# First three projection chains interleaved over K, memory products on three PSUM banks, the second remainder tile loaded in stage one

## The chip, the cores and the metric

The kernel runs on one NeuronCore of a Trainium2 chip. Its metric is the device time of that core in microseconds (us). A core has a matrix engine (TensorE, in the profile PE, with its weight loads as PEld), a vector engine (VectorE, DVE), an activation engine (ScalarE, ACT), a general engine (GpSimd, POOL), and a queue from which this kernel issues all its transfers (SyncE, SP). SBUF is the working memory. PSUM holds the matrix results: eight banks, each of 128 partitions by 512 float32 numbers.

## The reference, cut to what matters

The input `x` has 2048 rows and 576 columns. Two results are made from it and mixed row by row with `g = sigmoid(x . gate_w)`:

```
q, k, v = x @ wq, x @ wk, x @ wv            # 32 heads of 18, four segments of 512 rows
for each segment s:
    a_dot = softmax(q k^T * scale + causal mask) v      # inside the segment
    a_mem = (phi(q) M) / (phi(q) z + 1e-6)              # memory of the segments before
    M, z += phi(k)^T v, sum phi(k)
    o = sigmoid(beta) * a_mem + (1 - sigmoid(beta)) * a_dot
a = o @ wo
b = (silu(x @ w_gate) * (x @ w_up)) @ w_down            # 4608 hidden units
out = g * a + (1 - g) * b
```

The kernel computes float32 products from pairs: a number is split into a high part (a copy on ACT in a rounded type) and a low part (the difference, on DVE), and a product is high*high + high*low + low*high.

## The kernel before, in words

Every engine runs its instructions in the order in which the program lists them; the order of the work is written out by hand. A tile has a name, and each name has a fixed place (or a few, used in turn). A new tile under a name waits until the last reader of the tile that lay there is done. PSUM is used under eight names, `bank0` to `bank7`, and helpers such as `chain_tile = banks(0, 1, 2)` hand them out in turn.

Stage one goes through the four segments (`for s in range(NSEG)`, L562). A segment consists of two phases.

- **Nine chains** (L565, `qk`, L315). A chain makes 128 columns of q or k for the 512 rows of the segment. The 576 input columns are five K blocks (`NT = 5`; the last block is a half one that holds high and low part together). A chain is 14 matmuls of 512 columns into one bank (`products`, L134): three for each of four blocks, two for the last. Chain 0 to 4 are the (m, 0), chain 5 to 8 the (m, 1). When a chain is done it is evacuated: ACT copies it to 16 bits (L320), for some chains ACT makes `phi` from it (L325, L326), DVE takes the rest (L327), `mid` work follows, ACT copies the rest (L330), POOL takes what then is left (L331), and for the `phi` chains DVE reads the bank once more (L333). That last read frees the bank. The result is stored to DRAM two chains later (`flush`, L312).
- **Eight V steps** (L623, `v_step`), each of 14 matmuls of 288 or 290 columns, on banks 5, 6 and 7. From the second segment on a **memory step** (`mem_step`, L410) follows each V step: six short matmuls into one bank taken from `pair_tile = banks(3, 4)`, and four DVE instructions (L424 to L428) that read it. Between the chains of these segments `upd_gen` (L367) updates the memory M, with its sums in the same two banks.

At the very start the weights of chain 0 (all five blocks, 320 KB) are loaded, then x block by block (five transfers of 256 KB), then the weights of chain 1, 2, 3 and so on. ACT and DVE split weights and x in that order; the weights of chain n + 3 are split inside the evacuation of chain n. While the first data is on its way, nine matmuls on zeros run on PE (L437).

Stage two (from L659) is the feed-forward part in two halves of 36 steps f, with the attention heads worked in between. Its step makes seven products (`seven`) on `a_tile` (bank 0), `x_tile` (bank 1) and `y_tile` (bank 2); the first is on bank 0, the second on bank 2. Each product ends with one matmul (L1014) on a remainder tile `rh` that `r_fetch(f)` (L234) loads from DRAM; there are two such tiles. `r_fetch(0)` is issued in the last segment of stage one, the others inside stage two, one step ahead, from a list that is worked off beat by beat.

Few lines say how the memory step takes its bank:

```
            t = pair_tile([P, 16, E])                       # L417, mem_step
            acc = [pair_tile([P, 3, MW]), pair_tile([P, 2, MW])]   # L368, upd_gen
    y_tile = banks(2)                                       # L109
```

## Time and profile before

| what | value |
|---|---|
| median of three runs | 1793.36 us (1793.08 to 1793.77) |
| the profiled execution's own time | 1792.96 us |
| its span, first to last instruction | 1791.2 us |
| PE busy | 1775.8 us (99%) |
| DVE, ACT, POOL busy | 1268.9, 959.3, 830.9 us |
| stage one | about 0 to 222 us |
| granted TensorE clock | 1.00 |

All times inside the profile count from the first instruction of the span. A row of the timeline gives start, duration, engine, line of the kernel, operation, output and inputs, and in brackets how long the engine sat idle before it and what released it. `xcount` tells how many instructions were merged into the row. Matmuls overlap: one of 512 columns has a duration of 0.39 us, while a new one starts each 0.23 us. So a stall of PE is read from the starts of rows rather than from the busy share.

### The profile page before, as it was taken

The page shows a single profiled execution, that of the slowest core. Times are in us where ns is not written, and L with a number is a line of the kernel's source. Part 1 is how long each engine was busy: PE and PEld are TensorE (multiplying, and loading weights), DVE is VectorE, ACT ScalarE, POOL GpSimd, SP SyncE. Part 2 cuts the span into 40 slices and gives each one's busy share as a digit, 9 for nine tenths or more (in the row PEclk, how much of TensorE's full clock was granted, in tenths as well). Part 3 has the DMA queues.
Part 4 walks back from the last instruction along what each step waited for, and adds up shares of the span by engine and source line. Part 5 has one row for each costly group of instructions (what it writes and reads, how often), then busy time and mean ns, then how long its engine had stood idle before and what let it go on. Part 6 is the DMA issues. An engine that isn't in the chain of part 4 may idle for free.

```text
span 1791.2 us, 36353 instructions
## 1 busy us (share of the span) xinstructions
PE 1775.8 (99%) x12445; PEld 1525.6 (85%) x12445; DVE 1268.9 (71%) x3245; ACT 959.3 (54%) x1787; POOL 830.9 (46%) x1065
## 2 busy tenths in 40 slices
PE   9999999999999999999989999999999999999999
PEld 7899978888888888888877887887887887888899
DVE  6657566877877777777777777777777777764455
ACT  7766565465645564556446455455455455454511
POOL 4434731444554455444545555555555555553111
PEclk9999999999999999999999999999999999999999
DMA  8645496677757765676487456456455556456644
GB/s 291 217 175 183 150 342 215 194 252 263 228 168 249 248 220 167 230 247 235 138 277 238 144 152 207 131 160 198 149 163 177 147 161 194 138 147 194 198 135 140
DMA packets 242505, 352.01 MB, mean 197 GB/s; under 512 B 83408, under 2 KB 123728, under 8 KB 242320
## 3 DMA queue, kind: packets, MB, share of 16 engines
q1 hardware_dynamic: 242320, 349.68, 60.5%
q8 instruction: 99, 1.62, 0.4%
q14 instruction: 86, 0.70, 0.1%
HBM read 210.72 MB, written 138.87 MB: 195 GB/s over the span
## 4 chain that ended last, share of the span: by engine, by line
PE 93%; DVE 3%; ACT 1%; DMA 1%; issue 1%; SPq 0%; POOL 0%; ACTq 0%; DVEq 0%
PE bank L1011 37%; PE bank L870 24%; PE bank L136 11%; PE bank L1014 6%; PE bank L746 4%; PE bank L704 4%; PE bank L775 2%; PE bank L777 1%; DVE xo L114 1%; PE bank L375 1%; PE bank L421 1%; PE bank L929 0%; DMA rh<-rc 0%; PE bank L383 0%; DMA xo<-in_xT_dram 0%
## 5 line engine op out<-in xcount | busy, mean ns | idle before, releaser
L870 PE MATMUL bank<-dw,hh 128*128 128x320 f32 (+1 forms) x2304 | 486.5, 304 | 6.5 <-DVE ya L875 4.8
L840 POOL TENSOR_TENSOR p<-pe,p 128x512 f16<-128x512 f32 x320 | 382.9, 1197 | 154.2 <-DVE p L838 105.8
L870 PEld LDWEIGHTS bank<-dw,hh 128*128 128x128 f32 x2304 | 377.9, 189 | 25.3 <-DVE ya L875 6.7
L750 ACT ACTIVATE pe<-bank 128x512 f32<-128x512 f32 x320 | 190.3, 595 | 314.5 <-PE bank L746 285.7
L870 PE MATMUL bank<-dw,hl 128*128 128x320 f32 (+1 forms) x1152 | 340.2, 295 | 0.3 <-DVE hl L114 0.3
L758 POOL TENSOR_SCALAR_AFFINE_SELECT pe<-pe 128x256 f32<-128x256 f32 (+1 forms) x320 | 137.3, 429 | 292.7 <-ACT pe L750 288.9
L711 DVE CUSTOM_DVE_ANT_0 scr<-bank,cm 128x512 bf16<-128x512 f32 (+3 forms) x512 | 248.0, 484 | 20.0 <-PE bank L704 12.0
L875 DVE TENSOR_TENSOR ya<-bank,ya 128x320 f32<-128x320 f32 x352 | 158.0, 453 | 113.9 <-PE bank L870 111.6
L870 PEld LDWEIGHTS bank<-dw,hl 128*128 128x128 f32 x1152 | 217.6, 189 | 0.9 <-DVE hl L114 0.9
L1014 PE MATMUL bank<-xr,rh 128*128 128x512 f32 x504 | 196.7, 390 | 1.1 <-DMA rh<-rc 1.1
L838 DVE CAST p<-pe 128x512 f16<-128x512 f32 x320 | 152.3, 476 | 0.0
L746 PE MATMUL bank<-qst,kst 111*128 111x512 bf16 (+3 forms) x512 | 150.9, 303 | 0.0
L704 PE MATMUL bank<-kst,qst 108*128 108x512 bf16 (+3 forms) x512 | 126.0, 300 | 0.5 <-DVE mb L711 0.5
L245 POOL TENSOR_TENSOR ws<-raw 128x256 f32<-128x256 f32 x72 | 66.0, 916 | 109.5 <-DMA raw<-in_wf_dram 52.9
L954 DVE TENSOR_TENSOR hl<-row,hh 128x512 fp32r<-128x512 f32 x120 | 99.4, 829 | 20.8 <-ACT hh L953 20.4
L1014 PEld LDWEIGHTS bank<-xr,rh 128*128 128x128 f32 x504 | 94.6, 188 | 21.7 <-issue 1.5
L1077 ACT ACTIVATE row<-bank 128x512 f32<-128x512 f32 x72 | 43.1, 598 | 122.2 <-PE bank L1014 122.2
L1082 DVE TENSOR_TENSOR row<-bank,row 128x512 f32<-128x512 f32 x72 | 49.8, 691 | 80.8 <-ACT bank L1081 80.8
L1092 DVE TENSOR_TENSOR row<-bank,row 128x512 f32<-128x512 f32 x72 | 49.7, 690 | 64.0 <-PE bank L1014 51.7
L1081 ACT ACTIVATE bank<-bank 128x512 f32<-128x512 f32 x72 | 41.9, 582 | 96.6 <-PE bank L1014 93.5
L136 PE MATMUL bank<-xo,qhi 128*128 128x512 f32 x288 | 91.7, 398 | 0.8 <-DVE xo L114 0.8
L775 PEld LDWEIGHTS <-p 128*128 128x128 f16 x1280 | 69.1, 96 | 10.3 <-issue 6.6
(1691 smaller groups left out, 4006.4 us busy)
## 6 DMA issues: line engine op xcount, KB each, us to landing
rh<-rc SPq DMA_DIRECT2D x72, 336.0 KB
dc<-dw SPq DMA_DIRECT2D x36, 576.0 KB
dw<-dc SPq DMA_DIRECT2D x36, 576.0 KB
raw<-in_wf_dram SPq DMA_DIRECT2D x72, 256.0 KB
stk<-q SPq DMA_DIRECT2D x32, 384.0 KB
draw<-in_wd_dram SPq DMA_DIRECT2D x36, 288.0 KB
rc<-rt SPq DMA_DIRECT2D x42, 224.0 KB
vd<-vps SPq DMA_DIRECT2D x8, 912.0 KB
```

The source lines that it names most:

```text
L136: nc.tensor.matmul(t, st[n], mv[n], start=(n == 0), stop=(n == 13))
L704: nc.tensor.matmul(t[:, c:c + w], qs[:KR, pr, P * i:P * i + P], ks[:KR, pr, 0:w], start=True, stop=True)
L711: nc.vector.tensor_tensor_reduce(scr[:, :w], t[:, c:c + w], cm[:, L - w:L], 1.0, -3.0e38, OP.add, OP.max, m[:, k:k + 1])
L746: nc.tensor.matmul(t[:, c:c + w], ks[:KR + 3, pr, P * j:P * j + P], qs[:KR + 3, pr, P * j:L], start=True, stop=True)
L750: nc.scalar.activation(pe, t, AF.Exp, scale=SCALE)
L758: nc.gpsimd.affine_select(d, d, pattern=pat, compare_op=OP.is_ge, fill=0.0, base=0, channel_multiplier=-1)
L838: nc.vector.tensor_copy(p1, pe)
L840: nc.gpsimd.tensor_sub(p2, pe, p1)
L870: nc.tensor.matmul(t, p, q[:, cs], start=(n == 0), stop=(n == 3 * CH - 1))
L875: nc.vector.tensor_add(ya[:, i, cs], t, ya[:, i, cs])
L1011: nc.tensor.matmul(t, w[:, p, z], x[z][:, q], start=first and n == 0, stop=False, skip_group_check=True)
L1014: nc.tensor.matmul(t, rem[:, RPOS[j]], XR[j], start=False, stop=True, skip_group_check=True)
```

## The change

Three edits.

1. **The first three chains side by side.** Instead of all weights of chain 0 ahead of x, each of the five K blocks brings one transfer with this block of the weights of chains 0, 1 and 2 (192 KB in pieces of 512 bytes), followed by x's transfer of the same block. A new function `trio` walks over the blocks: it splits the three small weight tiles and x's block and issues the matmuls of this block for all three chains, on three banks. The evacuations of the three chains then follow. The first segment's chains take their banks from five (0 to 4) in turn instead of three. The weights of chains 3 and 4 are loaded directly behind the ten transfers, the split of chain 3's weights stands behind `trio`, those of chains 4 to 8 are done in the evacuations of chains 1 to 5. There are eight matmuls on zeros instead of nine.
2. **Memory steps on three banks.** `mem_step` takes its bank from `mem_tile = banks(3, 4, 2)`. `upd_gen` stays on `pair_tile`.
3. **The second remainder tile in stage one.** `r_fetch(1)` is issued in the last segment's fifth V step, behind two weight loads, and leaves stage two's list.

```diff
+    first_tile = banks(0, 1, 2, 3, 4)
+    mem_tile = banks(3, 4, 2)
...
+        def trio():
+            ts = [first_tile() for _ in range(3)]
+            xk, xs = xs_of[0]
+            for kt in range(NT):
+                nc.scalar.activation(qw[0][0][0][:, kt], qraw[kt][:, 0], AF.Copy)
+                raw = xr[kt]
+                if kt < 4:
+                    split(xk[kt][:, 0], xk[kt][:, 1], raw)
+                else:
+                    xs_split(xs, raw)
+                for m in range(3):
+                    if m:
+                        nc.scalar.activation(qw[m][0][0][:, kt], qraw[kt][:, m], AF.Copy)
+                    nc.vector.tensor_sub(qw[m][1][0][:, kt], qraw[kt][:, m], f32(qw[m][0][0][:, kt]))
+                for p, q in ((0, 0), (0, 1), (1, 0)) if kt < 4 else ((0, 0), (1, 0)):
+                    for m in range(3):
+                        nc.tensor.matmul(ts[m], qw[m][p][0][:, kt], xk[kt][:, q] if kt < 4 else xs,
+                                         start=(kt == 0 and p + q == 0), stop=(kt == 4 and p == 1))
+            return ts
+
         def qk(s, m, u, mid=()):
-            t = chain_tile()
-            hi, lo = qw[m]
-            products(t, w_stat(hi[u], lo[u]), x_side(*xs_of[s]))
+            if first:
+                t = first.pop(0)
+            else:
+                t = chain_tile() if s else first_tile()
+                hi, lo = qw[m]
+                products(t, w_stat(hi[u], lo[u]), x_side(*xs_of[s]))
...
-            t = pair_tile([P, 16, E])
+            t = mem_tile([P, 16, E])
...
-        q_load(0, 0)
...
-        for _ in range(9):
+        for _ in range(8):
...
-        xr = []
+        qraw, xr = [], []
         for kt in range(NT):
             if kt % 2 == 0:
-                pair = staging()
-            raw = pair[:, L * (kt % 2):L * (kt % 2) + L]
+                both = staging(), staging()
+            a = both[0][:, L * (kt % 2):L * (kt % 2) + 3 * P].rearrange("p (m n) -> p m n", n=P)
+            nc.sync.dma_start(a, wf[FT:FT + 3, :, 0, kt].rearrange("m p n -> p m n"))
+            qraw.append(a)
+            raw = both[1][:, L * (kt % 2):L * (kt % 2) + L]
             nc.sync.dma_start(raw, xT[0, :, kt])
             xr.append(raw)
...
-        q_load(*chains[1])
...
-        q_split(0, 0)
-        for kt in range(NT):
-            x_split(xs_of[0], kt, xr[kt])
-        q_load(*chains[2])
         q_load(*chains[3])
-        q_split(*chains[1])
-        q_split(*chains[2])
+        q_load(*chains[4])
+        first = trio()
+        q_split(*chains[3])
...
-        loads = {0: [lambda: q_load(*chains[4]), lambda: q_load(*chains[5])], 1: [lambda: q_load(*chains[6])],
+        loads = {0: [lambda: q_load(*chains[5])], 1: [lambda: q_load(*chains[6])],
...
-                    if n + 3 < 9:
+                    if 0 < n < 6:
                         mid.append(lambda n=n: q_split(*chains[n + 3]))
...
-                        if n == 3:
-                            r_fetch(0)
+                        if 3 <= n < 5:
+                            r_fetch(n - 3)
...
-                plan.append((1 if nxt[1] else 10, lambda f=nxt[1]: r_fetch(f)))
+                if nxt != (0, 1):
+                    plan.append((1 if nxt[1] else 10, lambda f=nxt[1]: r_fetch(f)))
```

## The prediction

> **What bounds the kernel now.** I read the page first: the span, the busy shares, the clock, the chain that ended last.

> ```profile
> span 1791.2 us, 36353 instructions
> PE 1775.8 (99%) x12445; PEld 1525.6 (85%) x12445; DVE 1268.9 (71%) x3245; ACT 959.3 (54%) x1787; POOL 830.9 (46%) x1065
> PE 93%; DVE 3%; ACT 1%; DMA 1%; issue 1%; SPq 0%; POOL 0%; ACTq 0%; DVEq 0%
> ```

> PE is the bound: 99% busy, 93% of the chain. The matmuls stay the same in number and size, so the change can gain only PE's idle time and lose only by new idle time. Next I read PE's own waits.

> ```profile
> PE bank L1014 <- DMA rh<-rc: 1.1, 1, 1.1
> PE bank L136 <- DVE xo L114: 0.8, 3, 0.3
> PE bank L421 <- DVE q L428: 0.8, 1, 0.8
> ```

> Of these, part 1 of the change aims at the second, part 2 at the third, part 3 at the first. They sum to 2.7 us, so there is little to win, and each new wait weighs. I go through the timeline at the four places that matter: the start, the end of segment 0, the first memory step of segment 2 (from 0), and the seam of stage one and two.

> **The start (trio).** PE's rows, the SP row of x's transfers, the splits on ACT and DVE, and the transfer rate of the first 30 us in slices of 0.75 us:

> ```profile
> 1.26 4.02 PE L437 MATMUL bank<-cm 128*128 128x512 bf16 x9 [1.26 <-DVE cm L434]
> 5.20 0.59 PE L136 MATMUL bank<-xo,qhi 128*128 128x512 f32 x1
> 13.93 0.61 PE L136 MATMUL bank<-xo,qhi 128*128 128x512 f32 x2
> 17.10 0.62 PE L136 MATMUL bank<-xo,qhi 128*128 128x512 f32 x2
> 1.25 2.31 SPq L443 DMA_DIRECT2D xo<-in_xT_dram  x5
> 5.97 0.63 ACT L113 ACTIVATE xo<-xo 128x512 fp32r<-128x512 f32 x1 [0.82 <-DMA xo<-in_xT_dram]
> 5.39 0.68 DVE L114 TENSOR_TENSOR xo<-xo,xo 128x512 fp32r<-128x512 f32 x1
> 213.31 0.40 ACT L249 ACTIVATE wo__2460<-raw 128x256 fp32r<-128x256 f32 x1
> 217.95 0.41 DVE L252 TENSOR_TENSOR wo__2460<-raw,wo__2460 128x256 fp32r<-128x256 f32 x1
> GB/s 0 0 89 276 365 311 240 259 356 397 394 396 403 413 413 394 380 368 274 106 283 238 284 337 319 422 396 370 348 363 410 299 46 20 385 200 16 10 1 127
> ```

> A chain runs 17.10 - 13.93 = 3.17 us, 0.227 us for each of 14 matmuls. Three chains need 9.5 us, and now take 11.9 us (5.20 to 17.10), because chain 0 waits for each x block. In trio a block brings 9 matmuls, 2.04 us of PE, for 192 + 256 KB = 459 kB, which at the 240 to 365 GB/s of 2.25 to 6 us take 1.3 to 1.9 us: less than PE needs. SP issues a transfer per 2.31/5 = 0.46 us, 0.92 us per block; also less. ACT has one x copy (0.63 us) and three small ones, at most 0.40 each by the row of twice their size: under 1.83 us. DVE likewise, under 0.68 + 3 x 0.41 = 1.91 us. So PE paces trio. I let its first matmul stand at 5.20 (a smaller first transfer gives 0.2 us back, the lost warm-up matmul costs nothing while PE waits for x); it ends at 5.20 + 9.5 = 14.7 instead of 17.10: 2.4 us ahead. The weights now arrive in pieces of 512 bytes; nothing in the busy start shows their price. Bounds: as shown, or half rate, 2.3 us per block, which puts 1 us on the end. I take the first, since even 20% slower still hides behind PE.

> **What of it survives segment 0.** Three banks now finish within 0.5 us, and ACT and DVE evacuate them one by one.

> ```profile
> 14.13 0.60 ACT L320 ACTIVATE q<-bank 128x512 bf16<-128x512 f32 x1 [1.01 <-PE bank L136]
> 15.48 0.63 ACT L330 ACTIVATE q<-qr 128x512 bf16<-128x512 f32 x1
> 20.48 0.60 ACT L320 ACTIVATE q<-bank 128x512 bf16<-128x512 f32 x1 [1.12 <-PE bank L136]
> 23.70 0.60 ACT L320 ACTIVATE q<-bank 128x512 bf16<-128x512 f32 x1 [0.67 <-issue]
> 26.87 0.60 ACT L320 ACTIVATE q<-bank 128x512 bf16<-128x512 f32 x1 [0.27 <-issue]
> 30.20 0.57 ACT L320 ACTIVATE q<-bank 128x512 bf16<-128x512 f32 x1
> 49.58 1.85 PE L136 MATMUL bank<-vw,xo 128*128 128x290 f32 x12 [0.15 <-DVE gl L355]
> ```

> One evacuation holds ACT from its first copy to the end of its last: 15.48 + 0.63 - 14.13 = 1.98 us, of which the overlap of rows takes 0.1; the weight split of the next chain fits into its inner wait. The first copy can start at 14.7 + 0.2 - 0.45 = 14.45 (0.2 behind the next chain's start as 14.13 stands to 13.93, and two matmuls earlier). Three pitches of 1.9 put the fourth at 20.15, where it is at 20.48 now: ACT has caught up with almost nothing. From there ACT's work without its idle time is 3.22 - 0.67, 3.17 - 0.27 and 3.33 us, so the seventh starts at 28.9 instead of 30.20. From there ACT and DVE run without a break up to the V step at 49.58, which waits for DVE: PE gains 1.3 us there, not 2.4. The range is 0.3 (trio late by 1 us) to 2.0 (tighter pitches).
> Chain 3 has its weights (split behind trio's copies). Chain 4's split stands behind the second copy: 14.45 + 1.9 + 0.60, and 0.79 for 640 columns (0.63 x 640/512), is 17.7; PE needs it at 14.7 + 3.17 = 17.9. Chain 4 is just served. SP issues ten transfers ahead of chain 3's, and chain 0's store waits for POOL some 3 us longer, with the loads for chain 8 and V behind it; they are split from 27 us on, so these 3 us are covered.

> **Memory steps.** The bank of a memory step is its running number modulo 3 in (3, 4, 2). Segment 1 takes numbers 0 to 7, segment 2 begins with number 8: bank 2. Chain 8 of every segment lies on bank 2 as well (ninth of three in turn). So segment 2's first memory step waits for the last read of its own segment's chain 8.

> ```profile
> 145.48 0.43 PE L136 MATMUL bank<-vw,xs 128*128 128x288 f32 x2
> 145.75 0.83 PE L421 MATMUL bank<-Mm,ph 128*128 128x152 f32 x6
> 148.34 0.82 PE L421 MATMUL bank<-Mm,ph 128*128 128x114 f32 x6
> 151.23 0.90 PE L421 MATMUL bank<-Mm,ph 128*128 128x152 f32 x6 [0.17 <-DVE om L428]
> 144.11 2.80 DVE L522 TENSOR_TENSOR xr<-xo,xr 32x512 fp32r<-32x512 f32 x1
> 148.25 0.68 DVE L522 TENSOR_TENSOR xr<-xo,xr 32x512 fp32r<-32x512 f32 x1
> 148.96 0.69 DVE L333 SCALAR_TENSOR_TENSOR ph<-bank,ph 128x512 f32<-128x512 f32 x1
> 150.63 0.46 DVE L428 TENSOR_TENSOR om<-bank,dn 128x288 f32<-128x288 f32 x1
> ```

> L333 at 148.96 is that read. It ends at 149.65; with 0.14 us from release to start (150.63 + 0.46 to 151.23) the step starts at 149.79 instead of 145.75. All V and memory steps queue behind it on PE. Two steps of 2.59 us later (148.34 - 145.75) the third comes at 154.97 instead of 151.23: +3.7 us, its own wait of 0.17 already given back. Nothing later in the segment waits, so the loss stays. In segment 1 the bank comes up at the third step, in segment 3 at the second, when chain 8 has been read.

> **The seam.** Segment 3's third memory step no longer waits. But the last one is number 23: bank 2 again, and bank 2 is `y_tile`, the second product of stage two.

> ```profile
> 208.77 0.90 PE L421 MATMUL bank<-Mm,ph 128*128 128x152 f32 x6 [0.77 <-DVE q L428]
> 222.04 0.41 ACT L349 ACTIVATE vf<-bank 128x288 f32<-128x288 f32 x1 [0.47 <-PE bank L136]
> 225.94 0.46 DVE L428 TENSOR_TENSOR q<-bank,dn 128x288 f32<-128x288 f32 x1
> 224.16 1.52 PE L1011 MATMUL bank<-xo,wo__2462 128*128 128x512 f32 x6
> 227.34 1.85 PE L1011 MATMUL bank<-xo,wo__2545 128*128 128x512 f32 x6
> 236.63 0.47 PE L1014 MATMUL bank<-xr,rh 128*128 128x512 f32 x1 [1.09 <-DMA rh<-rc]
> 236.93 1.53 PE L1011 MATMUL bank<-xo,wo__2734 128*128 128x512 f32 x6
> 230.00 0.85 SPq L235 DMA_DIRECT2D rh<-rc  x1
> ```

> That bank is read until 226.40 (225.94 + 0.46), after PE wants it at 224.16. PE, 0.8 us earlier, moves this read by at most the 0.47 us that ACT waits for it; I take 0.3. So the product starts at 226.25, +2.1 us. Then it goes on at 1.59 us a product ((227.34 - 224.16)/2) without the two old stalls: the seventh product after it starts at 226.25 + 7 x 1.59 = 237.4 where 236.93 stands now. Net +0.5 us over the seam. The remainder tile's wait would be gone by the delay alone; `r_fetch(1)`, some 10 us earlier on SP (0.85 us of SP saved at 230.00, spent ahead of the attention's first loads), gains nothing more. Bounds: -1.1 (no bank wait) to +1.0.

> **Sum.** -1.3 + 3.7 + 0.5 = +2.9 us on the profiled 1792.96 us, whose run lies 0.4 us below the median of 1793.36: 1796.3 us, +0.16%. Call 0.2% (3.6 us) what a measurement of this kernel can tell from no change: the forecast is within it, towards slower.

> **Rivals.**
> A. PE is idle from 145.91 to 149.79, 3.9 us, and falls back to the pace of the start: the nine warm-up matmuls take 4.02 us, 0.43 each, against 0.227 later, though the row below gives a clock of 1.00 there too. Four us at half pace lose 1.9 us: +4.8 us, 1798.2. It decides from the idle length at which PE falls back; no idle time of such length is in this trace.

> ```profile
> 0.00:5.00 5.00, 3.74 (x9) 1.19 (x9) 0.79 (x3) 2.41 (x3) 2.51 (x11) 1.00 0.64 182
> ```

> In that row of the first 5 us the counts are those of PE, PEld, DVE, ACT and POOL; 1.00 is the granted clock.
> [...]
> B. The front gains nothing: the small pieces or ACT's queue eat the 1.3 us. Then +4.2 us, 1797.6. For it: ACT and DVE are already the bound up to 49.58. Against it: the block's bounds all lie under PE's.
> C. Bank 2 is free earlier: DVE's row at 144.11 took 2.80 us where the same operation takes 0.68 at 148.25. Without these 2.1 us chain 8's last read ends at 147.5, and the sum is +0.8 us, 1794.2.
> [...] Against C: up to there all engines shift together, in the same order.
> D. The change only does what it says, and neither bank wait appears: -1.3 - 0.2 - 0.8 - 1.1 = -3.4 us, 1790.0. Against it: the two numbers, 8 and 23.

> **Chances.** Forecast 0.48 (own range +1.9 to +3.9, that is 1795.3 to 1797.3), A 0.20, B 0.16, C 0.11, D 0.05. A and B are slower by over 0.2% nearly always, the forecast in a fifth of its cases: slower 0.43, faster 0.03, same 0.54. The range goes from C's lower side to A's upper: 1793.9 to 1798.9.

> **What would show it.** Right: L421 in segment 2 starts with about 4 us of idle PE released by DVE L333; the second product of stage two waits some 2 to 3 us for DVE L428; no wait for rh; the fourth chain starts near 14.7 and the V step now at 49.58 near 48.3. Matmuls of 0.43 us pitch behind the first stall speak for A. Wrong if the first memory step of segment 2 starts without a wait, or if trio's matmuls stand with gaps for transfers.

## The result and the profile after

The changed kernel takes 1804.05 us (median of six runs, 1803.06 to 1807.28), the kernel before 1793.34 us (six runs). The ratio is 1.0064, interval 1.0054 to 1.0074: slower by 10.7 us. The forecast was 1796.3 us, the range ended at 1798.9. A loss was forecast, but too small by 7.8 us.

The page of the profile after: the span, the busy shares, the chain that ended last.

```profile
span 1803.0 us, 36363 instructions
PE 1779.1 (99%) x12444; PEld 1529.7 (85%) x12444; DVE 1269.7 (70%) x3257; ACT 960.0 (53%) x1799; POOL 832.3 (46%) x1065
PE 92%; DVE 2%; DMA 2%; ACT 2%; issue 1%; SPq 0%; POOL 0%; ACTq 0%; DVEq 0%
```

PE does the same matmuls and stays the bound. It is busy 3.3 us longer and idle 8.5 us longer (1803.0 - 1779.1 = 23.9, before 1791.2 - 1775.8 = 15.4). So the 11.8 us of the span (the profiled executions took 1804.74 and 1792.96 us) are of two kinds: new waits, and matmuls that take longer. PE's waits come first (what waits, on what; sum, count and longest in us):

```profile
PE bank L446 <- DVE ph L358: 3.9, 1, 3.9
PE bank L1034 <- DVE q L453: 3.6, 1, 3.6
PE bank L138 <- DVE vf L378: 1.9, 1, 1.9
PE bank L1034 <- DVE bank L1098: 1.5, 1, 1.5
```

The first two are the bank waits of the forecast, 3.9 us as foreseen and 3.6 us instead of 2.1. The third was not foreseen. The old waits on `rh` (1.1 us) and on the memory step of segment 3 (0.8 us) are gone. Next PE's timeline of the changed kernel at the three places:

```profile
40.21 0.43 PE L138 MATMUL bank<-vw,xs 128*128 128x288 f32 x2
42.51 3.01 PE L138 MATMUL bank<-vw,xo 128*128 128x288 f32 x12 [1.87 <-DVE vf L378]
...
145.87 1.74 PE L138 MATMUL bank<-vw,xo 128*128 128x288 f32 x12
147.45 0.43 PE L138 MATMUL bank<-vw,xs 128*128 128x288 f32 x2
151.76 1.43 PE L446 MATMUL bank<-Mm,ph 128*128 128x152 f32 x6 [3.89 <-DVE ph L358]
153.00 2.91 PE L138 MATMUL bank<-vw,xo 128*128 128x288 f32 x12
...
234.16 2.90 PE L1034 MATMUL bank<-xo,wo__2487 128*128 128x512 f32 x6 [3.59 <-DVE q L453]
237.28 1.58 PE L1034 MATMUL bank<-xo,wo__2534 128*128 128x512 f32 x6
```

Look at the durations behind each wait. Twelve matmuls of a V step take 1.74 us at 145.87, but 3.01 us at 42.51 and 2.91 us at 153.00; six of a product take 2.90 us at 234.16 and 1.58 us at 237.28. The same work takes nearly twice as long just behind a wait. The view of stretches says why (stretch, length, busy time and count of PE, PEld, DVE, ACT and POOL, then the granted clock, the DMA share and GB/s):

```profile
40.00:42.00 2.00, 0.64 (x5) 0.40 (x4) 2.00 (x5) 0.98 (x3) 1.25 (x1) 1.00 1.06 414
42.00:44.00 2.00, 1.50 (x7) 1.53 (x8) 1.18 (x3) 1.45 (x4) 0.93 (x3) 0.69 1.03 407
44.00:46.00 2.00, 2.00 (x10) 2.00 (x9) 1.54 (x3) 1.07 (x4) 0.57 (x1) 0.50 0.92 361
46.00:48.00 2.00, 2.00 (x16) 2.00 (x16) 1.49 (x3) 1.08 (x3) 0.73 (x1) 0.96 0.09 37
```

The granted clock is 0.50 behind the wait, and comes back at about 46 us. In the trace's records of that clock, half clock begins at 42.75, 151.98 and 233.90 us and lasts 3.41 us each time; before the change there is none between the start and the end of the kernel.

The ledger: how much later (+) the same matmul starts after the change than before it, read from the two timelines at the end of each place. The first row is part of the second.

| place | forecast | measured | of which half clock |
|---|---|---|---|
| end of trio (17.10, now 15.60) | -2.4 | -1.5 | |
| segment 0 in all (to the V step at 49.58, now 51.62) | -1.3 | +2.0 | 1.6 |
| first memory step of segment 2 (145.75, now 151.76) and the V step behind it | +3.7 | +5.2 | 1.5 |
| from segment 3's third memory step (208.77) to behind `rh`'s old wait (236.63, now 246.65) | +0.5 | +2.8 | 1.5 |
| the rest of stage two | 0 | +1.7 | |
| sum | +2.9 | +11.7 | 4.6 |

### The profile page after: what moved, and what is told of

Its sections match the earlier page's. It is cut to its first block, busy times and chain, and to the rows that moved or that the text cites. A ratio compares the mean times of both kernels' runs of the same rounds, so it can differ in the third digit from the quotient of the medians.

```text
span 1803.0 us, 36363 instructions
## 1 busy us (share of the span) xinstructions
PE 1779.1 (99%) x12444; PEld 1529.7 (85%) x12444; DVE 1269.7 (70%) x3257; ACT 960.0 (53%) x1799; POOL 832.3 (46%) x1065
## 4 chain that ended last, share of the span: by engine, by line
PE 92%; DVE 2%; DMA 2%; ACT 2%; issue 1%; SPq 0%; POOL 0%; ACTq 0%; DVEq 0%
PE bank L1034 36%; PE bank L893 25%; PE bank L138 11%; PE bank L1037 6%; PE bank L769 4%; PE bank L727 4%; PE bank L798 2%; PE bank L800 1%; PE bank L446 1%; PE bank L400 1%; DMA wo__23682<-wc 0%; DVE xo L116 0%; DMA stk<-q 0%; PE bank L332 0%; DMA raw<-in_xT_dram 0%
## 5 line engine op out<-in xcount | busy, mean ns | idle before, releaser
L138 PE MATMUL bank<-xo,qhi 128*128 128x512 f32 x264 | 83.1, 396 | 0.0
L1098 DVE TENSOR_TENSOR bank<-bank,row 128x512 f32<-128x512 f32 x72 | 50.2, 697 | 41.6 <-PE bank L1037 33.4
```

Source lines behind the costliest of these rows:

```text
L138: nc.tensor.matmul(t, st[n], mv[n], start=(n == 0), stop=(n == 13))
```

## The experiments

Ratios are to the kernel before on the same chip, where its medians were 1791.84 (e1 to e4), 1792.58 (e5 to e7 and the changed kernel once more) and 1792.31 us (e8 to e10 and e6 again).

**Theories.** T1: the order in which the memory steps take their banks makes two new waits, and behind each the granted clock halves; the front's gain does not survive segment 0, because something there holds it up. Rivals: three chains ahead or the early rests cost time by themselves; or the loss is the waits alone and the clock has little to do with it (the forecast).

**e1: memory steps back on two banks.**

```diff
-    mem_tile = banks(3, 4, 2)
+    mem_tile = pair_tile
```

> The changed kernel with its memory steps back on banks 3 and 4; trio and the early remainder tile stay. Theory (bank 2 makes two waits, and PE's clock halves after each): both waits, 3.89 and 3.59 us, and both slow stretches of some 1.6 us go, the old 0.9 us wait of segment 3's third memory step returns: 1804 - 5.4 - 3.6 + 1.0 = about 1796 us. What is left over before is segment 0's loss of about 2 us. Rival (the time went elsewhere, the waits only replace other ones): 1801 us or more.

1793.11 us, ratio 1.0005 (0.9996 to 1.0014): all but about 1 us is back with one line. Neither bank wait is there, and the granted clock is 1.00 throughout. The median is 3 us lower than expected; most of it is that segment 0 lost less here, in a profile of the shortest of the ten runs (1791.54 us). ACT's and PE's rows of e1:

```profile
29.89 0.60 ACT L345 ACTIVATE q<-bank 128x512 bf16<-128x512 f32 x1 [0.25 <-DMA stk<-q]
...
41.22 1.83 PE L138 MATMUL bank<-vw,xo 128*128 128x288 f32 x12 [0.84 <-DVE vf L378]
```

The V step waits 0.84 us instead of 1.87, at full clock (12 matmuls in 1.83 us). The bracket of ACT's row gives a hint of why; here is the same row after the change, with SP's rows that issue the first stores and the chain's piece from issue to landing; the last two rows are SP's before the change:

```profile
31.18 0.60 ACT L345 ACTIVATE q<-bank 128x512 bf16<-128x512 f32 x1 [1.49 <-DMA stk<-q]
...
18.60 0.33 SPq L314 DMA_DIRECT2D stk<-q  x1
23.16 2.39 SPq L314 DMA_DIRECT2D stk<-q  x2
...
23.16 7.94 DMA stk<-q
...
14.39 0.33 SPq L312 DMA_DIRECT2D stk<-q  x1
20.63 0.34 SPq L312 DMA_DIRECT2D stk<-q  x1
```

ACT's first copy for chain 6 needs the buffer from which chain 2 is being stored (`q3` has four). That store is issued at 23.16, where it was issued at 20.63 before the change: chain 0 is done only when chains 1 and 2 nearly are, the first store leaves at 18.60 instead of 14.39, and the others behind it. It lands 7.94 us later, at 31.1, amid the loads for V. In e1 it is issued at 22.91 and ACT goes on at 29.89, so the landing differs from run to run by more than the issue. ACT waits 1.49 us, DVE and ACT stand late for the rest of the segment, and the V step at 42.51 waits for them.

**e2: chain 6 in a buffer of its own**, a slot among x's tiles, so that ACT need not wait for that store.

```diff
-            q3 = sp.tile([P, 3, L], BF, name="q3", bufs=4)
+            if (s, m, u) == (0, 1, 1):
+                q3 = xo.tile([P, 4, L], BF, name="xo50")[:, 0:3]
+            else:
+                q3 = sp.tile([P, 3, L], BF, name="q3", bufs=4)
```

> The changed kernel, but chain 6 of segment 0 writes its 16-bit parts into another, free place, so that it needs no old one back. Theory (ACT waits 1.5 us there for chain 2's store, which lands late since SP issues it late behind loads; this pushes the V step's wait to 1.87 us and halves PE's clock): the wait of the first copy of chain 6 goes, the fourth V step waits 0.4 us or less, the clock stays at 1.00 there, about 3 us less: 1801 us. Rival (ACT and DVE are simply behind because three evacuations come at once): ACT's wait goes, but DVE stays late and PE still waits over 1 us; 1803 us or more.

1802.79 us, ratio 1.0061 (1.0044 to 1.0077). ACT's wait is gone, the V step near 40 us waits 0.24 us, and there is no half clock in segment 0. But the slot was wanted again:

```profile
42.60 0.63 ACT L115 ACTIVATE xo<-xo 128x512 fp32r<-128x512 f32 x1 [1.11 <-DMA stk<-xo]
```

The split of x for segment 1 waits for chain 6's own store out of that slot, and PE in turn 0.63 us at 44.84. Segment 0 still ends 0.3 us earlier than before the change instead of 2.0 us later. The median did not follow: about 1801 us was expected, and the ratio is hardly below the changed kernel's 1.0064. One reason is that in this run the half clock in segment 2 lasted 6.83 us, two periods, and that segment cost 6.2 us in place of 5.2. Another is that segment 0 of the changed kernel itself does not always lose so much (see the run behind e4). So the wait for the store is what held segment 0 up; what it is worth in the median is not shown by e2.

**e3: PE kept busy through the waits**, with 7, 14 and 14 matmuls on zeros ahead of the three waiting matmuls. Their results are used by nothing.

```diff
+    def fill(n, *ids):
+        t = banks(*ids)()
+        for _ in range(n):
+            nc.tensor.matmul(t, cm[:, 0:P], cm, start=True, stop=True)
...
+            if (s, hf, i) == (0, 0, 3):
+                fill(7, 0)
...
+            if (s, i, bank) == (2, 0, 0):
+                fill(14, 0)
...
+            if pos == 0:
+                fill(14, 3)
```

> The changed kernel with matmuls on the zeros or the mask tile put ahead of the three waits (7 ahead of segment 0's fourth V step, 14 ahead of segment 2's first memory step, 14 ahead of the second product of stage two), each group shorter than the wait that it stands in; their results are used by nothing. Theory (the slow matmuls behind the waits come from the clock that PE's idleness lowers): the granted clock stays at 1.00 in all three places, each stretch gets 1.5 to 1.7 us back, about 1799.2 us, with the waits' ends where they were. Rival (the first matmuls after a wait are slow because DVE or ACT still work on PSUM, or for want of weights): the same slow stretches, 1804 us.

1800.75 us, ratio 1.0045 (1.003 to 1.006). The stalls stay as long (a filler and a rest of 0.8 and 0.6 us take their place), yet no half clock follows at the three places. The filler (L117) and the V step of segment 0, and the rests of the two long waits:

```profile
40.75 1.68 PE L117 MATMUL bank<-cm 128*128 128x512 bf16 x7
42.09 1.94 PE L143 MATMUL bank<-vw,xo 128*128 128x288 f32 x12
...
PE bank L455 <- DVE ph L363: 0.8, 1, 0.8
PE bank L1043 <- DVE q L462: 0.6, 1, 0.6
```

The twelve matmuls take 1.94 us in place of 3.01. In segment 2 the lateness grows by 3.7 us in place of 5.2, at the seam by 1.2 in place of 2.8. By the ratios (1.0045 against 1.0064 and, below, 1.006) this gives back 2.7 to 3.4 us, though the intervals overlap. Some of the 4.6 us was lost again: 1.3 us near 330 us, and 1.1 to another half clock, at 918.25 us, behind two waits of 0.86 and 1.29 us in the attention heads:

```profile
914.00:918.00 4.00, 2.05 (x13) 1.60 (x13) 3.47 (x6) 1.55 (x3) 2.23 (x2) 1.00 0.87 279
918.00:921.70 3.70, 3.70 (x16) 3.27 (x17) 0.99 (x3) 0.45 (x1) 1.95 (x2) 0.54 1.05 411
```

So half clock is a cause by itself: the stalls remain, it goes from their places, and the lateness that it had brought there goes with it.

**e4: the kernel before with memory steps on three banks, nothing else.**

```diff
+    mem_tile = banks(3, 4, 2)
...
-            t = pair_tile([P, 16, E])
+            t = mem_tile([P, 16, E])
```

> The kernel before with the memory steps on banks 3, 4, 2 and nothing else of the change. Theory: the two waits with their slow stretches come back here: +5.4 us in segment 2, -1.0 us in segment 3, +3.6 us at the seam, with the old wait for the remainder tile hidden behind the new one: 1793.3 + 8.0 = about 1801.3 us. Rival (the waits need the shift that trio brings): under 1797 us.

1801.14 us, ratio 1.0051 (1.0036 to 1.0066). PE's waits, and the stretches of segment 2 and of the seam:

```profile
PE bank L422 <- DVE ph L334: 3.9, 1, 3.9
PE bank L1012 <- DVE q L429: 2.9, 1, 2.9
```

```profile
149.00:152.00 3.00, 2.48 (x10) 2.51 (x11) 1.45 (x6) 0.67 (x2) 1.56 (x2) 0.50 0.76 249
152.00:155.70 3.70, 3.70 (x19) 3.70 (x17) 0.59 (x2) 0.73 (x2) 0.00 (x0) 0.50 0.47 188
...
232.60:236.00 3.40, 3.40 (x15) 2.84 (x16) 1.70 (x4) 0.90 (x2) 0.74 (x1) 1.00 0.71 280
```

This one edit brings 9.3 us, where the whole change cost 10.7. Behind the wait of 3.9 us the clock is halved for 6.83 us; behind that of 2.9 us it stays at 1.00.

**The changed kernel once more**, on the chip of the next two.

> The changed kernel once more, to stand beside the two versions below on the same chip. If the three waits (DVE vf L378 near 42 us, DVE ph L358 near 148, DVE q L453 near 230) and a half clock of 3.413 us behind each are the cause: again 10 to 12 us over the kernel before, ratio 1.0055 to 1.0065. If the place of the clock's windows decides much of it, which differs from run to run: the two long waits stay at 3.6 to 3.9 us, but the number of half-clock windows behind them changes, and the time lies 6.5 to 12 us above.

1802.86 us, ratio 1.006 (1.0045 to 1.0075). The two long waits are again 3.9 and 3.6 us. In segment 0 ACT waits 0.3 us for the store and PE 0.9 us, without half clock; in segment 2 half clock lasts 6.83 us. Segment 0 ends 0.9 us ahead of before, segment 2 costs 6.3 us, the seam 2.8 and the rest of stage two 0.4. The places change, the total hardly.

**e5: the memory steps still on three banks, but counted anew in each segment**, so that bank 2 falls to steps 3 and 6 of eight.

```diff
-    mem_tile = banks(3, 4, 2)
+    mem_banks = [banks(3), banks(4), banks(2)]
...
-            t = mem_tile([P, 16, E])
+            t = mem_banks[(2 * i + bank) % 3]([P, 16, E])
```

> The changed kernel, memory steps still on three banks, but counted anew in each segment, so that bank 2 falls to the third and sixth of the eight memory steps and never to the first after chain 8 nor to the last before stage two. Theory (the order of the banks costs the time, not the third bank): no wait for DVE ph L358 and none of over 1 us for DVE q L453 at the seam, no wait for rh, no half clock in segment 2 or at the seam; as with the memory steps on two banks (1.0005 there), less the 0.8 us that the two banks wait in segment 3: ratio 0.9990 to 1.0003, that is -1.8 to +0.5 us. Rival (three chains ahead and the second rests cost time by themselves): 1.002 or more, with the loss ahead of 50 us or in stage two.

1794.1 us, ratio 1.0009 (0.9999 to 1.0019). Neither bank wait, no half clock: the order of the banks made the loss, not their number. But the ratio is 0.6 thousandths over the upper end of the expectation. The gain of 1.0 us at segment 3's third memory step was given back at the seam:

```profile
225.75 1.66 PE L1034 MATMUL bank<-xo,wo__2534 128*128 128x512 f32 x6 [0.96 <-ACT bank L1091]
...
225.12 0.57 ACT L1091 ACTIVATE bank<-bank 128x512 f32<-128x512 f32 x1
```

The third product of stage two waits for ACT's copy of the first one, and that copy stands behind the end of segment 3 on ACT, at 225.12 (224.84 before the change). PE came earlier, ACT didn't. From there to its end the profiled run lost another 3.0 us net, part of it in waits for this copy (0.43, 0.79 and 0.84 us near 315, 422 and 553 us) where ACT had itself waited 0.9 to 1.6 us for transfers; it was one of the longest runs of e5 (1796.19 us of 1792.37 to 1796.44).

**e6: e5, and chain 6 in another slot among x's tiles.**

```diff
-            q3 = sp.tile([P, 3, L], BF, name="q3", bufs=4)
+            if (s, m, u) == (0, 1, 1):
+                q3 = xo.tile([P, 4, L], BF, name="xo61")[:, 0:3]
+            else:
+                q3 = sp.tile([P, 3, L], BF, name="q3", bufs=4)
```

> As the one before, and chain 6's 16-bit parts in segment 0 go into a buffer of their own among x's, which frees ACT from waiting for chain 2's store. Theory (ACT's wait for that store eats the front's gain): ACT has no wait at its copy near 30 us, PE's wait for the V parts near 41 us falls from 0.8 to 1.9 to 0.3 us or less, segment 0 ends 0.5 to 1 us earlier than in the version before, ratio 0.9985 to 0.9995. Rival (the x buffer is wanted again by the next segment's split before the store has read it): a wait of about 0.6 us near 44 us takes its place and nothing is gained, ratio as before to within 0.0003.

1792.12 us, ratio 0.9999 (0.999 to 1.0009). ACT's wait for the store is gone and none for x's slot takes its place; the V step near 41 us waits 0.3 us, and PE is 1.0 us ahead behind segment 0; 2.0 us are gained on e5's median, though the intervals overlap. The theory's range ended at 0.9995. The same kernel again:

> The version with three chains ahead, banks counted anew in each segment, chain 6 in a buffer of its own and the second rests fetched early, once more, beside the parts above on the same chip. Theory (it keeps 1 us of the front, 0.8 us of the third bank and 1.1 us of the rests, of which the seam takes 1 back; later waits for transfers take up to 1 more): 1.0 to 2.0 us faster than before, ratio 0.9989 to 0.9995. Rival (what is gained ahead of 240 us is lost in stage two from run to run): 0.9996 to 1.0003.

1792.26 us, ratio 0.9997 (0.9988 to 1.0006), again above the theory's range, which ended at 0.9995. PE stands 2.4 us ahead at 206 us, 1.3 behind the same wait for ACT at the seam (0.97 us), 2.3 when `rh`'s old wait is passed, and 1.7 at the end.

**e7: idle times of eight lengths** between bursts of 48 matmuls, set by fills of SBUF on DVE, ahead of the kernel before; nothing uses its results, and it adds some 450 us.

```diff
+        flat = vf.rearrange("p a h e -> p (a h e)")
+        nc.vector.memset(cm, 0.0)
+        for gap in (0, 2100, 900, 3900, 300, 2700, 1500, 3300) * 4:
+            t = lone_tile()
+            for _ in range(48):
+                nc.tensor.matmul(t, cm[:, 0:P], cm, start=True, stop=True)
+            nc.vector.memset(cm, 0.0)
+            if gap:
+                while gap > 0:
+                    nc.vector.memset(flat[:, :min(gap, 2400)], 0.0)
+                    gap -= 2400
+                nc.vector.memset(cm, 0.0)
```

> The kernel before with a prelude that nothing uses: bursts of 48 matmuls, with PE idle between them for eight lengths from about 0 to 4 us, four times over; it adds some 400 us. Theory A (the clock halves when a window of 3.413 us, which runs on whatever the kernel does, holds too little work, not only none at all): half clock follows some idle times of 1.9 to 3.4 us and not others of the same length, always for a multiple of 3.413 us, and nearly all of those over 3.5 us. Theory B (a whole window must be idle): no half clock after any idle time under 3.4 us; always one after 6.8 us, sometimes one between.

In its one run, half clock came behind all twelve idle times of 3.67 us and more, behind three of four of 2.30 us, one of four of 2.92, and none of 1.67 or less. Two of 2.3 us, the idle stretch and the burst behind it:

```profile
97.60:99.90 2.30, 0.03 (x1) 0.03 (x2) 1.85 (x3) 0.00 (x0) 0.00 (x0) 1.00 0.00 0
99.90:103.50 3.60, 3.60 (x10) 1.25 (x11) 0.00 (x0) 0.00 (x0) 0.00 (x0) 0.53 0.02 5
...
323.50:325.80 2.30, 0.04 (x1) 0.04 (x2) 1.85 (x3) 0.00 (x0) 0.00 (x0) 1.00 0.00 0
325.80:329.40 3.60, 3.60 (x17) 1.64 (x18) 0.00 (x0) 0.00 (x0) 0.00 (x0) 1.00 0.02 5
```

The same idle time, once with 10 matmuls behind it in 3.6 us, once with 17. All changes of the clock lie on one grid of 3.413 us. Against that grid the rows fall in order: the clock halved where 2.12 us or more of the idle time fell into one period, and not where at most 1.95 did (the 2.92 that were split 1.51 + 1.41, 1.17 + 1.75 and 1.67 + 1.25; the 2.30 split 1.95 + 0.34). The wait of 2.9 us at e4's seam, which half clock did not follow, was split 1.17 + 1.75 as well. In all profiles, half clock lasted one period where the next one held up to 0.26 us of idle time, and two where it held 0.62 or more. Theory A stands; theory B, a whole idle period, falls.

**e8: the early rests alone**, in the kernel before.

```diff
-                        if n == 3:
-                            r_fetch(0)
+                        if 3 <= n < 5:
+                            r_fetch(n - 3)
...
-                plan.append((1 if nxt[1] else 10, lambda f=nxt[1]: r_fetch(f)))
+                if nxt != (0, 1):
+                    plan.append((1 if nxt[1] else 10, lambda f=nxt[1]: r_fetch(f)))
```

> The kernel before with the second rests fetched in stage one, and nothing else of the change. Theory (the wait for rh was a real gap on PE's path and nothing else stands close behind it): the wait of 1.1 us near 236 us is gone, no new one at the seam, since PE comes there at the same time as before; PE 1.1 us earlier from there on, ratio 0.9992 to 0.9997 (some of it goes to waits for transfers later in stage two). Rival (the gain is given back in stage two altogether, which is paced by its transfers): ratio 0.9998 to 1.0003.

1792.06 us, ratio 0.9991 (0.9982 to 1.0). The wait on `rh` is gone, and nothing takes its place at the seam. The medians lie only 0.25 us apart and the interval ends at 1.0, so a gain in the total is not shown. In the profile PE is 1.6 us ahead behind it, 0.3 of which stood there from the first 17 us on, where nothing was changed, and 0.55 at the end; so some is given back in stage two.

**e9: the three chains alone** (against the changed kernel):

```diff
-    mem_tile = banks(3, 4, 2)
+    mem_tile = pair_tile
...
-                        if 3 <= n < 5:
-                            r_fetch(n - 3)
+                        if n == 3:
+                            r_fetch(0)
...
-                if nxt != (0, 1):
-                    plan.append((1 if nxt[1] else 10, lambda f=nxt[1]: r_fetch(f)))
+                plan.append((1 if nxt[1] else 10, lambda f=nxt[1]: r_fetch(f)))
```

> The kernel before with the first three chains side by side, and nothing else of the change: memory steps on two banks, second rests as before. Theory (the front's gain of 1.5 to 2.2 us at 15 us is used up by the V step near 41 us, where PE waits 0.3 to 1.9 us for parts that ACT and DVE make, and ACT waits for chain 2's store): from 50 us on PE is 0 to 1 us earlier than before and the ratio 0.9997 to 1.0005. Rival (the forecast's: 1.3 us of the front survive to the end): 0.9990 to 0.9994.

1794.43 us, ratio 1.0009 (1.0 to 1.0018): above the theory's range, which ended at 1.0005. The front's gain is used up, and by the medians the edit costs 2 us, though the interval begins at 1.0. PE is 1.5 us ahead at 15.6, and 0.3 us late at 42, where ACT's and PE's waits stand again:

```profile
PE bank L138 <- DVE vf L378: 1.3, 1, 1.3
...
ACT q L345 <- DMA stk<-q: 1.0, 1, 1.0
```

The profiled run stands 0.24 us ahead at 236 us (the wait on `rh` shrinks when PE comes later) and 1.0 us late at the end, lost in short waits of stage two (0.62 us at 552, 0.98 at 901). Why these come with an earlier front was not found.

**e10: e8's edit, and memory steps counted anew as in e5**; the start as before.

```diff
+    mem_banks = [banks(3), banks(4), banks(2)]
...
-            t = pair_tile([P, 16, E])
+            t = mem_banks[(2 * i + bank) % 3]([P, 16, E])
```

> The kernel before with memory steps on three banks, counted anew in each segment, and the second rests fetched in stage one; the start as before. Theory: segment 3's wait of 0.77 us at the third memory step is gone, and the rh wait of 1.1 us too; but PE, 0.8 us ahead at the seam, waits there 0.4 to 1.0 us for ACT, whose evacuation of the first product stands behind the end of segment 3, so that 1.0 to 1.5 us are left at 240 us; ratio 0.9990 to 0.9997. Rival (the third bank alone costs something, as in the changed kernel): a wait for DVE ph of over 1 us in a segment, half clock behind it, ratio over 1.002.

1791.23 us, ratio 0.9992 (0.9984 to 1.0001), the lowest median of all. PE is 1.95 us ahead at segment 3's third memory step (0.6 of it from the first 17 us, where nothing was changed), loses 0.35 at the seam (a wait of 0.3 us for ACT) and is 2.3 ahead at the end. Its median lies 1.1 us below the kernel before; the interval still holds 1, so that it beats it is likely and not shown.

The wait in segment 0 can be followed through the profiles with the three chains ahead (without e3, where a filler stands in that wait):

| profile | ACT waits for chain 2's store | PE waits at the V step near 41 us | PE behind segment 0, late (+) against before |
|---|---|---|---|
| e2 (buffer of its own; x's split waits) | 0 | 0.24 | -0.3 |
| e6, e6 again (buffer of its own) | 0 | 0.3, 0.3 | -1.0, -1.0 |
| e1 | 0.25 | 0.84 | -0.4 |
| changed kernel once more | 0.3 | 0.9 | -0.9 |
| e5 | 0.8 | 1.2 | +0.3 |
| e9 | 1.0 | 1.3 | +0.4 |
| changed kernel | 1.49 | 1.87, then half clock | +2.0 |

The profile before, against which the last column stands, has itself a late start: at 17 us e4, e8 and e10, where the start is the same, stand 0.25, 0.3 and 0.6 us ahead of it. So these leads are too large by some tenths; the differences between the rows are not touched by that.

## Why the prediction was wrong, step by step

**The premise failed.** "The matmuls stay the same in number and size, so the change can gain only PE's idle time and lose only by new idle time": the same matmuls took longer. PE was busy 3.3 us more. Behind the waits the granted clock was 0.50, and the ledger puts 4.6 us down to it, a term that the sum had at nothing.

**The start: right in kind, 0.9 us off.** Trio ends at 15.60, not 14.7: 1.5 us ahead. The step "PE paces trio" failed in part; the changed kernel's rows there:

```profile
7.92 1.69 PE L332 MATMUL bank<-xo,qhi 128*128 128x512 f32 x6 [0.54 <-ACT xo L115]
15.60 0.61 PE L138 MATMUL bank<-xo,qhi 128*128 128x512 f32 x2
```

PE waited 0.54 us for x's split. In the other profiles trio ended between 14.86 and 15.86, so it varies from run to run by as much as the miss. The clock has a part in it: full clock is recorded from 5.21 us on here, where the first six matmuls took 1.78 us, from 4.41 in the second profile of the changed kernel, where they took 1.69, and only from 7.04 in e9, where they took 2.61.

**What survives segment 0: the first step of the path that failed.** "SP issues ten transfers ahead of chain 3's, and chain 0's store waits for POOL some 3 us longer ... so these 3 us are covered" looked at the loads behind the store and forgot the stores themselves: what a store frees is a buffer, and chain 6 needs chain 2's. I named the queue and not who waits for its buffers. In place of -1.3 us stood +0.8 at that V step (the wait of 1.87 us, less a lead of 1.1), and +2.0 with half clock. e2 and e6 show it: without that wait segment 0 ends earlier than before the change. How much it costs differs: in the five profiles of the table with chain 6 in its old buffers, segment 0 ended between 0.9 us ahead and 2.0 us late, and in none the 1.3 us ahead that were forecast.

**Segment 2: the wait sized right, its consequence not.** Idle 3.89 us where 3.9 was worked out from L333's row, the long row of DVE included, which took 2.80 us again, so rival C fell:

```profile
146.08 2.80 DVE L545 TENSOR_TENSOR xr<-xo,xr 32x512 fp32r<-32x512 f32 x1
148.89 0.69 DVE L358 SCALAR_TENSOR_TENSOR ph<-bank,ph 128x512 f32<-128x512 f32 x1
```

The term missing from the sum is rival A's, half clock behind the stall, priced at 1.9 us and given 0.20. It cost 1.5 us here, and some 2.6 in the second profile, where it lasted two periods; and it was held to one place, where the seam had it as well, and in this profile segment 0.

**Rival A was left out of the sum for a weak reason.** "It decides from the idle length at which PE falls back; no idle time of such length is in this trace" was true, and spoke neither for it nor against it: there was no ground for counting on full clock. The runs showed it: in the records of the changed kernel half clock lasts 3.413 us each time, and from 5.206 us on its changes lie 37.547, 3.413, 105.813 and 3.413 us apart, which are 11, 1, 31 and 1 of such periods. The clock was halved there behind a wait of 1.87 us, and in e7 with 2.12 us of idle time in a period.

**The seam: wait 3.59 us, not 2.1.** The step "PE, 0.8 us earlier, moves this read ... I take 0.3" failed: the read did not move with PE at all. DVE's row of it in the changed kernel:

```profile
233.55 0.46 DVE L453 TENSOR_TENSOR q<-bank,dn 128x288 f32<-128x288 f32 x1
```

That is 7.6 us later than the 225.94 of before, while PE, its waits at segment 3's memory steps gone, came 6.3 us later. So the wait is the 2.24 us that stood between PE's wish and the read's end, and 1.3 on top. ACT's rows, before and after, show what the V steps there hang on:

```profile
215.31 0.42 ACT L249 ACTIVATE wo__2462<-ws 128x256 fp32r<-128x256 f32 x1 [1.60 <-POOL ws L245]
...
222.59 0.42 ACT L251 ACTIVATE wo__2487<-ws 128x256 fp32r<-128x256 f32 x1 [1.65 <-POOL ws L247]
```

Ahead of the copies for the V steps ACT copies a weight piece for stage two, and for that it waits for POOL, which is busy without a break from 208.12 (215.37 after) on. POOL was 7.3 us late, and ACT and DVE with it, where PE was 6.3; DVE lost another 0.35 us at 227.95 (220.33 before), which the profile does not explain. The prediction had looked only at ACT's wait of 0.47 us for PE. `rh`'s wait went as forecast, and half clock came on top.

**The rest of stage two, forecast as nothing, was +1.7 us:** 0.7 near 316 us and 1.3 at 901 us, less 0.3 won back at 912. PE's wait on L1098 at 901 goes back to ACT waiting 1.1 us for x from DRAM. Waits of this kind stand in every profile, at changing places (0.3 us at 901 before the change, 0.9 in e5), and in the second profile of the changed kernel the rest of stage two cost 0.4 us. So most of this term belongs to the one profile.

**What was right:** both bank waits named with their places and instructions, the sign, the end of the waits on `rh` and on segment 3's memory step, and rival D's fall. Rival B, that the front gains nothing, was nearer than the forecast's 1.3 us in four of the five profiles with chain 6 in its old buffers. Between the two profiles the sum was wrong by 8.8 us: segment 0 with its half clock 3.3, half clock in the two other places 3.0, the seam's wait 0.8, and the rest of stage two 1.7. In the second profile it was wrong by 5.8 us: segment 0 only 0.4, segment 2 with its two periods of half clock 2.6, the seam 2.3, the rest 0.4. What both have is the half clock in segment 2 and at the seam and the seam's longer wait; most of segment 0's part is of the first profile.

## What to carry to other kernels

A rotation over banks is to be followed through every user of those banks to the end of the count: one step too far, at the first turn after a late reader, cost here more than the whole change could win, and starting the count anew in each segment took the loss away. Price a new stall of PE of about 2 us and more with the half clock that may follow it (here it followed waits of 1.87, 3.59 and 3.89 us and cost 1.5 to 1.6 us for one period, about 1 us more for two), and look at all places where such a stall is new, not only the longest. Work that is moved ahead gains only up to the next engine that doesn't come earlier too (here ACT's wait for a store's buffer in segment 0, and ACT's wait for POOL ahead of the seam), so follow the stores, and who needs the buffers they free.
